# A fused attention and feed-forward kernel: the scores' bias product on 64 rows instead of 6, its query side held per tile of 128 tokens, and the planned order worked out again

## The chip, the cores and the metric

One core of one Trainium2 chip. The metric is device microseconds of one execution; the median of three executions of the kernel before is 662.76 us (662.45 to 664.29). PE is TensorE (its weight loads are told apart as PEld), DVE VectorE, ACT ScalarE, POOL GpSimd, SP SyncE, which here issues every DMA.

## What is computed

Causal attention with a forget bias, then two feed-forward layers with gates. The parts that matter, cut from the reference:

```python
# q, k, v: (4, 8, 576, 64), s: (4, 8, 576)
scores = scale * np.matmul(q, k.transpose(0, 1, 3, 2))
cum = np.cumsum(np.maximum(s, 0.0), axis=-1)
bias = -(cum[:, :, :, None] - cum[:, :, None, :])
scores = np.where(causal, -1000000000.0, scores + np.minimum(bias, 0.0))
attn = np.exp(scores - np.max(scores, axis=-1, keepdims=True))
attn = attn / (np.sum(attn, axis=-1, keepdims=True) + 1e-09)
x = np.matmul(attn, v)           # as (4 * 576, 512)
h = x @ w_in                     # 512 -> 1024
solu = h * softmax(h)            # then a layer norm times g_ln
y = ln(solu) @ w_out             # 1024 -> 512
h2 = np.maximum(np.maximum(y @ w1, y @ w2), y @ w3)   # 512 -> 768
out = h2 @ w_out2                # 768 -> 512
```

Products are made of f16 parts: a high and a low part of each side, three products of the four.

## The kernel before

Four batches go in two pairs; a pair has nine tiles: four blocks of 128 tokens of either batch (j = 0 to 3, batch c = 0 or 1), and one tile with the last 64 tokens of both, the tail. So there are 18 tiles, 0 to 17; tiles 8 and 17 are the tails. Two tiles make a group for the later layers, nine groups.

A tile goes through these steps. `prep` loads k, q and v, splits them into high and low halves (L417 and L419 the high half, L446 or on POOL L453 and L456 the low) and turns them, by DMA (L756, L766) or, for tiles 0 to 3, by TensorE with an identity (L486, L500). `scores` makes the scores of two heads at a time: head y of a pair uses rows 64y to 64y + 63 of TensorE, so the two run side by side. One step of it is the bias product (L832, both heads), and then three combinations of halves (L838). The bias is a product of 6 rows: three bf16 parts of the cumulative sum of the query side with ones, and ones with three parts of the key side. These rows stand in two buffers, `ckr` and `cqr`, of 128 x 4 x 576 bf16, at partitions 32c + 64y; both are filled with ones (or minus ones) by DVE (L557, L558) and then get their sums by DMA from `cum_d` (L596), eight loads a pair. A block of j = 0 has four steps in a row, of j = 1 two, of j = 2 and 3 one; a tail step makes four bias products, of 64 columns of weights each. Then come the minimum with the mask (L871, L906 in the tail), the exponential (L925), its halves (`es`), their turn by DMA (L952) into `et`, and `values` (L1009, in the tail L990 and L996), which ends in the scaling by the sums (L1043, L1037). Its result is split (`xs`) and turned (L1058) into `xt`.

`m1` is the product with w_in (L1082) and the normalisation (L1096, L1103, L1108, L1118, L1143 or L1144), which ends in halves `ln` and their turn (L1157) into `lnt`; buffers `e` and `ln` are single. `m2` is the product with w_out (L1179) and its two halves (L466 or L470, L1196), `m3` that with w1, w2, w3 and their maximum (L1218, L1237), `m4` that with w_out2 (L1252). The weights come as f32, are unpacked by DVE (L635, L641, L644) and split (L649, L659), which fills the first 150 us.

What sets the order: `Schedule.run` places every step on its engine with costs in ns, priorities `pos` made from the numbers in `P`, and a margin `look` within which the step of the lowest `pos` goes first. A step that can run on several engines goes where it would end first, by the margins in `spare`. The result is one fixed order for each engine; on the chip each engine takes its instructions in that order and waits by semaphores. Scores are forced into tile order (`in_turn`).

Of the kernel before, what the change touches and what calls it, by code (L numbers as in the profile page):

```python
# [32 lines left out]
P = dict(  # L33
    la=5.252,
    lp=-0.709,
    lu=-11.55,
    lv=-1.294,
    o1=-4.074,
    o2=-1.718,
    o3=-1.083,  # L40
    o4=-1.501,
    ds=2.623,
    wi=-17.396,
    wid=2.725,
    wo=-21.919,
    wod=-17.446,
    w3=14.089,
    w3d=1.947,
    w4=-21.45,
    w4d=16.108,  # L50
    mp=-2.793,
    look=[0.0, 0.0, 0.0, 1442.9, 54.8],
    spare=[1764.9, 1665.2, 1829.4, -777.9, -220.5, 1692.7, 26.2],
# [308 lines left out]
def build(nc, T, X, dims):  # L362
# [165 lines left out]
    def prologue():  # L528
# [29 lines left out]
        op([("DVE", 1100, lambda: nc.vector.memset(T["cqr"].bitcast(F32), MINUS_ONES))], [], ["cq1"], p0, kind="one")  # L558
# [29 lines left out]
    def load_c(p):  # L588

        unit(f"c{p}", f"c{p}")  # L590
        cd = T["cum_d"].rearrange("(b x y) i s -> b y i x s", b=B, y=2) if T else None
        for c in range(2):
            for name, of, n in (("ckr", "ck", 3), ("cqr", "cq", 0)):
                for y in range(2):
                    r0 = c * 32 + y * 64 + n
                    o = op([("SP", 450, lambda name=name, c=c, y=y, r0=r0: nc.sync.dma_start(  # L596
                        out=T[name][r0:r0 + 3], in_=cd[2 * p + c, y]))],
                       ["cum_d", of + "1"], [(of, c, y)], p * (2 * NB + 1) - P["la"] - P["lc"] + c * 0.2, dma=300, kind="c")
                    named[f"c{p}{c}"] = o
# [206 lines left out]
    def scores(t, h0):  # L806
# [73 lines left out]
        for n, (lo, hi) in enumerate(((0, KH), (KH, S))):  # L880
# [3 lines left out]
            def f_sc(n=n, lo=lo, hi=hi, sc=sc):  # L884
                steps = []
                for y in range(2):
                    for i in range(2):
                        cs = slice(i * 64, (i + 1) * 64)

                        def keys(x, r, i=i):  # L890
# [413 lines left out]
def fox_attention_solu_max3_kernel(  # L1304
# [110 lines left out]
```

## Time and profile before

| | |
|---|---|
| median of three executions | 662.76 us |
| the profiled execution: span | 661.9 us |
| PE busy | 620.3 us (94%) |
| DVE busy | 467.5 us (71%) |
| ACT busy | 299.6 us (45%) |
| POOL busy | 33.7 us (5%) |
| mean granted TensorE clock | 0.994 of full speed |

The page comes from one execution under the hardware profiler. Busy time of an engine is the union of its instructions' durations; products on PE are pipelined, so one that follows another starts before that one has ended. What a product costs the stream is therefore read from start to start. A row of a timeline merges neighbouring instructions of one kind: `x6` are six of them, and its duration runs from the start of the first to the end of the last. The number behind an idle engine's row is how long it was idle, and which instruction ended that.

### The profile page before, as it was taken

Reading aid. Unit: us, or ns where it says so; the run is one execution under the profiler, and the core shown is the slowest. Engines: PE = TensorE matmul, PEld = TensorE weight load, DVE = VectorE, ACT = ScalarE, POOL = GpSimd, SP = SyncE. Lnnn points to the kernel's source line nnn. Section 1 sums busy time; section 2 is a strip of 40 time slices with the busy share of each in tenths; the row PEclk is TensorE's granted clock in tenths of the full one; section 3 lists DMA queues with packets and bytes.
Section 4 is the critical chain, followed back from the end, with each engine's and each line's share of the span. In section 5 each row is a group of like instructions: output and inputs, shape, how many; then the busy total and the mean of one; then the engine's idle time right before and its main releaser. Section 6 shows DMA issues by size and latency. Waiting matters only on the chain.

```text
span 661.9 us, 15252 instructions
## 1 busy us (share of the span) xinstructions
PE 620.3 (94%) x6203; PEld 444.2 (67%) x6203; DVE 467.5 (71%) x1112; ACT 299.6 (45%) x712; POOL 33.7 (5%) x49
## 2 busy tenths in 40 slices
PE   3688978799999999999999999999999999999997
PEld 1344447577685567777577847785778577878684
DVE  7799999997697978696887668576884754513031
ACT  4687875464445555354743247325532514110100
POOL 1011100020000011020010001000000000000000
PEclk9999989899999999999999999999999999999999
DMA  6996866569988777898799674537663552100001
GB/s 171 279 248 163 207 192 172 163 111 173 176 158 135 148 129 129 132 142 164 142 195 173 129 130 105 94 72 112 124 102 65 109 69 49 34 33 1 33 1 32
DMA packets 249349, 82.66 MB, mean 125 GB/s; under 512 B 225472, under 2 KB 244096, under 8 KB 249280
## 3 DMA queue, kind: packets, MB, share of 16 engines
q1 hardware_dynamic: 249280, 81.70, 61.0%
q8 instruction: 48, 0.79, 0.5%
q14 instruction: 21, 0.17, 0.1%
HBM read 35.95 MB, written 4.83 MB: 62 GB/s over the span
## 4 chain that ended last, share of the span: by engine, by line
PE 71%; DVE 16%; issue 6%; DMA 3%; ACT 3%; SPq 0%; POOL 0%; DVEq 0%; POOLq 0%
PE acc L1218 27%; PE acc L1179 12%; PE acc L1252 10%; PE w L1082 9%; PE w L838 5%; PE av L1009 3%; DVE acc L641 2%; PE w L832 2%; DVE acc L644 2%; PE av L996 2%; DMA kt<-in_moe_w_in_dram 1%; DMA et<-es 1%; DVE r L871 1%; DVE f L635 1%; DVE w_h L659 1%
## 5 line engine op out<-in xcount | busy, mean ns | idle before, releaser
L1218 PE MATMUL acc<-x2A,w_h 128*128 128x256 f16 x1296 | 216.7, 274 | 3.2 <-DVE f L1237 1.1
L1218 PEld LDWEIGHTS <-w_h 128*128 128x128 f16 x1944 | 188.2, 98 | 32.9 <-issue 8.2
L1218 PE MATMUL acc<-x2B,w_h 128*128 128x256 f16 x648 | 177.2, 273 | 0.2 <-DVE x2B L1196 0.2
L925 ACT ACTIVATE r<-r,mn 128x128 f32<-128x128 f32 (+4 forms) x144 | 83.0, 578 | 59.4 <-DVE mn L871 48.2
L1082 PE MATMUL w<-w_in_h,xt 128*128 128x512 f16 x432 | 100.0, 383 | 1.4 <-DVE mn L871 1.2
L1179 PE MATMUL acc<-lnt,w_out_h 128*128 128x256 f16 x864 | 98.0, 273 | 1.0 <-DVE w_h L659 0.9
L1179 PEld LDWEIGHTS <-w_out_h 128*128 128x128 f16 x864 | 83.6, 98 | 13.1 <-issue 2.7
L1237 DVE TENSOR_TENSOR f<-f,acc 128x512 f32<-128x512 f32 x54 | 36.9, 683 | 68.0 <-PE acc L1218 68.0
L1082 PEld LDWEIGHTS <-xt 128*128 128x128 f16 x432 | 41.7, 98 | 50.1 <-issue 4.3
L1252 PE MATMUL acc<-w2o_h,h2A 128*128 128x512 f16 x216 | 64.4, 380 | 0.0
L446 DVE SCALAR_TENSOR_TENSOR es<-r,es 128x512 f16<-128x512 f32 (+1 forms) x89 | 59.8, 676 | 6.3 <-ACT es L417 4.6
L466 ACT ACTIVATE f<-acc 128x512 f32<-128x512 f32 x37 | 22.1, 596 | 85.5 <-PE acc L1218 51.6
L871 DVE CUSTOM_DVE_ANT_0 r<-w,mask 128x128 f32<-128x128 f32 (+3 forms) x128 | 57.7, 484 | 1.5 <-PE w L838 0.2
L838 PE MATMUL w<-kt,qt 64*128 64x256 f16 (+2 forms) x768 | 47.1, 262 | 0.2 <-ACT qt L503 0.2
L1103 ACT ACTIVATE ln<-e,st 128x1024 f32<-128x1024 f32 x18 | 20.7, 1147 | 49.8 <-DVE e L1096 44.5
L1252 PE MATMUL acc<-w2o_h,h2B 128*128 128x512 f16 x108 | 40.9, 379 | 0.0
L1009 PEld LDWEIGHTS <-et 128*128 128x128 f16 x960 | 34.7, 99 | 6.8 <-DMA et<-es 1.4
L1009 PE MATMUL av<-vs,et 128*128 128x64 f16 x960 | 36.4, 194 | 1.4 <-DMA et<-es 1.0
L838 PEld LDWEIGHTS <-qt 64*128 64x128 f16 (+1 forms) x864 | 26.6, 99 | 13.5 <-issue 6.4
L466 ACT ACTIVATE x2A<-acc 128x512 f16<-128x512 f32 x17 | 10.1, 595 | 55.0 <-PE acc L1179 55.0
L1252 PEld LDWEIGHTS <-h2A 128*128 128x128 f16 x216 | 19.6, 98 | 22.5 <-issue 2.1
L417 ACT ACTIVATE es<-r 128x512 f16<-128x512 f32 (+1 forms) x39 | 22.3, 575 | 23.9 <-DMA et<-es 20.9
(142 smaller groups left out, 730.9 us busy)
## 6 DMA issues: line engine op xcount, KB each, us to landing
kt<-in_moe_w_dram SPq DMA_DIRECT2D x18, 256.0 KB
vs<-in_moe_w_dram SPq DMA_DIRECT2D x18, 256.0 KB
raw<-in_k_dram SPq DMA_DIRECT2D x16, 256.0 KB
raw<-in_q_dram SPq DMA_DIRECT2D x16, 256.0 KB
raw<-in_v_dram SPq DMA_DIRECT2D x16, 256.0 KB
out_dram<-f SPq DMA_DIRECT2D x16, 256.0 KB
kt<-in_moe_w_out_dram SPq DMA_DIRECT2D x7, 512.0 KB
vs<-in_moe_w_out_dram SPq DMA_DIRECT2D x7, 512.0 KB
```

The source lines that it names most:

```text
L417: eng.activation(out=out(g), in_=src(g), func=AF.Copy, scale=sc(g))
L446: nc.vector.scalar_tensor_tensor(out=lo(g), in0=src(g), scalar=sc1(g), in1=hi(g), op0=ALU.mult, op1=ALU.subtract)
L466: nc.scalar.activation(out=out(*a), in_=in_(*a), func=AF.Copy, scale=scale)
L838: yield lambda n=n, qa=qa, o=o, kx=kx: nc.tensor.matmul(out=out()[:, o], lhsT=qv()[r, qa * HP + hp, ts], rhs=kx, start=False, stop=(n == 2 ...
L871: nc.vector.tensor_tensor_reduce(out=gw(R)[:, g], in0=gw(sc[y])[:, g], in1=T["mask"][:, SM - W:SM], scale=1.0 / S_MUL, scalar=3e38, op0=AL ...
L925: nc.scalar.activation(out=gw()[:, g], in_=gw()[:, g], func=AF.Exp, bias=mnf()[:, g:g + 1], scale=-1.0, accum_out=den(hs[g]),)
L1009: nc.tensor.matmul(out=out, lhsT=ea_[:, ea, kb], rhs=T["v_s"][c, kb // 2][:, kb % 2, ha + a, va], start=(kb == 0 and m == 0), stop=(kb == ...
L1082: nc.tensor.matmul(out=hb()[:, n * 512:(n + 1) * 512], lhsT=xt()[:, xa, kk], rhs=T["w_in_h"][:, wa, kk, n * 512:(n + 1) * 512], start=(kk ...
L1179: nc.tensor.matmul(out=ps()[:, d % 2 * GN:(d % 2 + 1) * GN], lhsT=T["w_out_h"][:, wa, kk, d * 128:(d + 1) * 128], rhs=lnt()[:, la, kk], st ...
L1218: nc.tensor.matmul(out=ps()[:, f % 2 * GN:(f % 2 + 1) * GN], lhsT=T["w123_h"][:, w, wa, f, kk], rhs=x2(xa)[:, kk], start=(kk == 0 and i == ...
L1237: op([("DVE", dve2(2 * GN), lambda ps=ps: nc.vector.tensor_tensor(out=m(), in0=m(), in1=ps(), op=ALU.max))], pk + [m], [m], pos, kind="m3x")
L1252: nc.tensor.matmul(out=ps(), lhsT=h2(ha)[:, f, o * 128:(o + 1) * 128], rhs=T["w2o_h"][:, wa, f], start=(f == 0 and i == 0), stop=(f == KF2 ...
```

## The change

The cumulative sums of the query side no longer stand for all 576 tokens of a pair. There are two buffers, `cq0` and `cq1`, one for each batch c of the pair, of 128 x 4 x 128 bf16. At the start POOL fills each with zeros, and rows 32c + 64y to 32c + 64y + 5 with minus ones. `load_cq` loads the three rows of sums for one tile: 128 tokens, or 64 in the tail; there are 40 such loads in place of 8. The bias product then takes rows 64y to 64y + 63 of `cq` and of `ckr`, 64 rows where it took 6; the rows beyond the six meet zeros. The planner's cost of a score step is 45 ns less, and all numbers in `P` that set the order are others, so that every engine's order differs from the old one. Of the steps that can run on several engines, POOL gets none any more.

```diff
-    look=[0.0, 0.0, 0.0, 1442.9, 54.8],
-    spare=[1764.9, 1665.2, 1829.4, -777.9, -220.5, 1692.7, 26.2],
+    look=[142.7, 33.8, 109.5, 156.1, 586.9],
+    spare=[1975.6, 1776.4, 6995.8, -4053.9, 1618.5, 1839.7, 112.3],
...
-        op([("DVE", 1100, lambda: nc.vector.memset(T["cqr"].bitcast(F32), MINUS_ONES))], [], ["cq1"], p0, kind="one")
+        for c in range(2):
+            op([("POOL", 400, lambda c=c: nc.gpsimd.memset(T["cq"][c].bitcast(F32), 0.0))],
+               [], [("cq", c, y) for y in range(2)], p0, kind="one")
+            for y in range(2):
+                r0 = 32 * c + 64 * y
+                op([("POOL", 400, lambda c=c, r0=r0: nc.gpsimd.memset(T["cq"][c][r0:r0 + 6].bitcast(F32), MINUS_ONES))],
+                   [], [("cq", c, y)], p0, kind="one")
...
+    def load_cq(t, pos):
+        p, c, j = tiles[t]
+        cd = T["cum_d"].rearrange("(b x y) i s -> b y i x s", b=B, y=2) if T else None
+        n = TL if c is None else 128
+        for i in ((0, 1) if c is None else (c,)):
+            for y in range(2):
+                r0 = i * 32 + y * 64
+                op([("SP", 450, lambda i=i, y=y, r0=r0: nc.sync.dma_start(
+                    out=T["cq"][i][r0:r0 + 3, :, 0:n], in_=cd[2 * p + i, y][:, :, j * 128:j * 128 + n]))],
+                   ["cum_d"], [("cq", i, y)], pos, dma=60, kind="cq")
...
             qb, qr, qk = load_tok("q", p, c, j, pos)
+            if j:
+                load_cq(t, pos)
...
             r = slice(64 * y, 64 * y + 64)
-            cr = slice(c0, c0 + 6)
             yield lambda: nc.tensor.matmul(
-                out=out(), lhsT=T["cqr"][cr, hp, cs], rhs=T["ckr"][cr, hp, ck], start=True, stop=False,
+                out=out(), lhsT=T["cq"][i][r, hp, 0:ts.stop - ts.start], rhs=T["ckr"][r, hp, ck], start=True, stop=False,
...
-            o = op([("PE", G * (pe(1, W) + pe(3 * nf, W / nf) + 60), f_sc)],
+            o = op([("PE", G * (pe(1, W) + pe(3 * nf, W / nf) + 15), f_sc)],
...
-    T["cqr"] = mk("cqr", [128, HP, S], BF16)
+    T["cq"] = [mk(f"cq{c}", [128, HP, 128], BF16) for c in range(2)]
```

How the order moves, at three places. The lines of the changed kernel stand some 20 further on: its L972 is the old L952, L777 the old L756, L742 the old L723, L1016 the old L996, L1102 the old L1082, L1238 the old L1218.

DVE at the very start, before and then after (`ckr` and `cqr` are the bias buffers, `k_tail` holds the identity there, `ln`, `e` and `lnt` the cumulative sums):

```order
L557 MEMSET ckr 128x1152
L558 MEMSET cqr 128x1152
L550 TENSOR_SCALAR k_tail<-k_tail 128x128 x5
L574 SCALAR_TENSOR_TENSOR e_106<-ln_107 32x576
L583 CAST lnt_108<-e_106 32x576
L582 TENSOR_TENSOR ln_107<-e_106,lnt_108 32x576
```

```order
L557 MEMSET ckr 128x1152
L550 TENSOR_SCALAR k_tail<-k_tail 128x128 x5
L580 SCALAR_TENSOR_TENSOR e_107<-ln_108 32x576
L589 CAST lnt_109<-e_107 32x576
L588 TENSOR_TENSOR ln_108<-e_107,lnt_109 32x576
```

The fill of the query side's buffer is gone from DVE; the sums follow one instruction sooner.

SP at the turns of tile 4's exponentials (`es` to `et`), before and then after; `raw` is what k, q and v are loaded to, `kt` the turned keys:

```order
L952 DMA_TRANSPOSE et_99<-es_93 128x6x128
L952 DMA_TRANSPOSE et_100<-es_94 128x6x128
L756 DMA_TRANSPOSE kt_71<-st_87 128x8x128
L723 DMA raw_84<-in_q_dram 128x8x64
L952 DMA_TRANSPOSE et_97<-es_93 128x6x128
L952 DMA_TRANSPOSE et_98<-es_94 128x6x128
```

```order
L972 DMA_TRANSPOSE et_100<-es_94 128x6x128
L972 DMA_TRANSPOSE et_101<-es_95 128x6x128
L742 DMA raw_85<-in_k_dram 128x8x64
L616 DMA cq_79<-cum_d 3x4x128 x2
L972 DMA_TRANSPOSE et_100<-es_94 128x6x128
L972 DMA_TRANSPOSE et_101<-es_95 128x6x128
L742 DMA raw_86<-in_q_dram 128x8x64
```

Two loads of the query side's sums, for tile 6, now stand between two pairs of turns.

PE behind the last values of tile 17, the last tile (`av` the values, `xt` the turned result of a tile, `w` the scores or the first layer, `acc` with `w_h` the three-way layer), before and then after:

```order
L996 LDWEIGHTS et_98
L996 MATMUL av_127<-vs_75,et_98 128x64
L1082 LDWEIGHTS xt_103
L1082 MATMUL w_126<-w_in_h,xt_103 128x512
...
L1218 LDWEIGHTS w_h
L1218 MATMUL acc_130<-x2A_110,w_h 128x256
```

```order
L1016 LDWEIGHTS et_99
L1016 MATMUL av_128<-vs_75,et_99 128x64
L1238 LDWEIGHTS w_h
L1238 MATMUL acc_130<-x2A_111,w_h 128x256
...
L1102 LDWEIGHTS xt_105
L1102 MATMUL w_127<-w_in_h,xt_105 128x512
```

Before, nine products of tile 16's first layer and 72 of the three-way layer stood ahead of tile 17's own first layer; after, 66 of the three-way layer.

## Rows read from the trace of the kernel before

**Rows 1.** the page, part 1: busy us (share of the span), xinstructions

```profile
PE 620.3 (94%) x6203; PEld 444.2 (67%) x6203; DVE 467.5 (71%) x1112; ACT 299.6 (45%) x712; POOL 33.7 (5%) x49
```

**Rows 2.** busy us in two stretches of the span, granted clock, DMA share, GB/s

```profile
0.00:150.00 150.00, 117.36 (x945) 74.03 (x946) 138.39 (x327) 100.36 (x236) 13.71 (x24) 0.98 0.71 190
150.00:540.00 390.00, 385.65 (x4290) 279.18 (x4289) 293.69 (x723) 180.66 (x440) 20.00 (x25) 1.00 0.74 131
```

**Rows 3.** the same for DVE alone, the densest ten microseconds

```profile
110.00:120.00 10.00, 9.96 (x20) 1.00 0.75 226
```

**Rows 4.** the chain of work that ended last: start us, us, what

```profile
625.97 23.58 PE acc L1218 x216
552.85 5.18 PE w L1082 x24
```

**Rows 5.** timeline of PE and its weight loads, four score steps: start us, us

```profile
318.60 0.28 PE L832 MATMUL w<-ckr,cqr 6*128 6x256 bf16 x2
318.81 0.50 PE L838 MATMUL w<-kt,qt 64*128 64x256 f16 x6
318.81 0.22 PEld L838 LDWEIGHTS <-qt 64*128 64x128 f16 x6
319.24 0.28 PE L832 MATMUL w<-ckr,cqr 6*128 6x256 bf16 x2
...
321.19 0.39 PE L1252 MATMUL acc<-w2o_h,h2A 128*128 128x512 f16 x1
```

**Rows 6.** timeline of PE near 59 us, f16 then f32 products

```profile
58.64 0.81 PE L1082 MATMUL w<-w_in_h,xt 128*128 128x512 f16 x3
59.28 0.60 PE L486 MATMUL acc<-k_tail,r 128*128 128x128 f32 x4
```

**Rows 7.** all of L832 from 150 us: count, ns min/median/max, starts, forms

```profile
L832 PE MATMUL w<-ckr,cqr x150: 224/318/385, 154.2 to 524.4; 6*128 6x512 bf16 x32, 6*64 6x256 bf16 x32, 6*64 6x320 bf16 x32, 6*128 6x384 bf16 x22
```

**Rows 8.** timeline of DVE, the fill of cqr

```profile
2.32 1.02 DVE L558 MEMSET cqr<- 128x1152 f32 x1 [0.19 <-issue]
```

**Rows 9.** timelines of POOL and SP; SP waits (total us, times, longest)

```profile
1.68 0.53 POOL L559 MEMSET mask<- 128x512 bf16 x1
13.21 0.59 SPq L596 DMA_DIRECT2D cqr<-cum_d  x2
SPq L952 <- DVE es L446: 70.3, 39, 10.6
```

**Rows 10.** timelines, tiles 17 and 7: last values on PE, issue of the turn

```profile
542.53 0.51 PE L996 MATMUL av<-vs,et 128*128 128x64 f16 x12
545.15 1.23 SPq L1058 DMA_TRANSPOSE xt<-xs  x1
248.82 0.78 PE L1009 MATMUL av<-vs,et 128*128 128x64 f16 x21
254.79 2.07 SPq L1058 DMA_TRANSPOSE xt<-xs  x1
```

**Rows 11.** the chain again: a turn from issue to landing

```profile
236.65 5.17 DMA et<-es
```

**Rows 12.** timelines: normalisation of tiles 5 and 17 to its turn; a landing

```profile
204.68 5.34 PE L1082 MATMUL w<-w_in_h,xt 128*128 128x512 f16 x24 [0.30 <-DVE mn L871]
232.77 1.71 SPq L1157 DMA_TRANSPOSE lnt<-ln  x1
558.06 1.22 DVE L1096 TENSOR_SCALAR_CACHE_REDUCE e<-w 128x1024 f32<-128x1024 f32 x1 [2.03 <-PE w L1082]
556.06 17.05 SPq L1157 DMA_TRANSPOSE lnt<-ln  x2
307.82 1.83 SPq L1157 DMA_TRANSPOSE lnt<-ln  x1
312.22 1.15 ACT L1103 ACTIVATE ln<-e,st 128x1024 f32<-128x1024 f32 x1 [5.27 <-DMA lnt<-ln]
```

**Rows 13.** waits of PE from 140 to 540 us: total, times, longest

```profile
PE w L832 <- DVE mn L906: 1.6, 1, 1.6
```

More of the change, by code (lines that the diff above doesn't have):

```diff
@@ L33 @@
 P = dict(
[L34 to L51, printed above, removed]
-    look=[0.0, 0.0, 0.0, 1442.9, 54.8],
-    spare=[1764.9, 1665.2, 1829.4, -777.9, -220.5, 1692.7, 26.2],
+    la=5.521,
+    lp=0.734,
+    lu=-45.556,
+    lv=1.446,
+    o1=-4.25,
+    o2=-2.859,
+    o3=-1.764,
+    o4=-1.319,
+    ds=0.164,
+    wi=-18.597,
+    wid=4.919,
+    wo=-12.688,
+    wod=-49.697,
+    w3=31.312,
+    w3d=5.865,
+    w4=-18.789,
+    w4d=42.619,
+    mp=-1.752,
+    look=[142.7, 33.8, 109.5, 156.1, 586.9],
+    spare=[1975.6, 1776.4, 6995.8, -4053.9, 1618.5, 1839.7, 112.3],
     n_st=4,
@@ L59 @@
     nr=3,
-    lat=2.304,
-    tp=0.396,
+    lat=2.777,
+    tp=0.872,
     wp=[0, 20, 20],
-    lc=-23.373,
+    lc=-35.216,
     S=[],
@@ L591, in load_c @@
         cd = T["cum_d"].rearrange("(b x y) i s -> b y i x s", b=B, y=2) if T else None
+        t = p * (2 * NB + 1)
         for c in range(2):
[L593 to L599, printed above, removed]
+            pos = t - P["la"] - P["lc"] + c * 0.2
+            for y in range(2):
+                r0 = c * 32 + y * 64 + 3
+                op([("SP", 450, lambda c=c, y=y, r0=r0: nc.sync.dma_start(out=T["ckr"][r0:r0 + 3], in_=cd[2 * p + c, y]))],
+                   ["cum_d", "ck1"], [("ck", c, y)], pos, dma=300, kind="c")
+            load_cq(t + c, pos)
+            named[f"c{p}{c}"] = S_.ops[-1]
+    def load_cq(t, pos):
[3 more added lines that the diff above has]
+        for i in ((0, 1) if c is None else (c,)):
+            for y in range(2):
+                r0 = i * 32 + y * 64
+                op([("SP", 450, lambda i=i, y=y, r0=r0: nc.sync.dma_start(
+                    out=T["cq"][i][r0:r0 + 3, :, 0:n], in_=cd[2 * p + i, y][:, :, j * 128:j * 128 + n]))],
+                   ["cum_d"], [("cq", i, y)], pos, dma=60, kind="cq")
     stage_keys = [
@@ L760, in prep @@
         qb, qr, qk = load_tok("q", p, c, j, pos)
+        if j:
+            load_cq(t, pos)
         qa = buf("st")
@@ L825, in scores, with products @@
         keyed = [(x, i, y) for x in ("ck", "cq") for i in ((0, 1) if tail else (c,)) for y in range(2)]
-        def products(out, y, h, ts, cs, keys, c0, ck):
+        def products(out, y, h, ts, keys, i, ck):
             hp = h // 2
             r = slice(64 * y, 64 * y + 64)
-            cr = slice(c0, c0 + 6)
             yield lambda: nc.tensor.matmul(
-                out=out(), lhsT=T["cqr"][cr, hp, cs], rhs=T["ckr"][cr, hp, ck], start=True, stop=False,
+                out=out(), lhsT=T["cq"][i][r, hp, 0:ts.stop - ts.start], rhs=T["ckr"][r, hp, ck], start=True, stop=False,
                 skip_group_check=True,
@@ L894, in f_sc @@
                         steps.append(products(
-                            lambda y=y, cs=cs: sc[y]()[cs, 0:hi - lo], y, h0 + y, cs, slice(SM, S),
-                            keys, 32 * i + 64 * y, slice(lo, hi),
+                            lambda y=y, cs=cs: sc[y]()[cs, 0:hi - lo], y, h0 + y, cs, keys, i, slice(lo, hi),
                         ))
```

3 lines of the change are left out of this document (1 added, 2 removed).

## The prediction

> **What bounds the kernel now.** I read the page first, then the busy times by stretch, then the chain of waits, then TensorE's timeline. PE is busy 94% of the 661.9 us, DVE 71%, ACT 45% [rows 1]. By stretch this splits in two [rows 2]: up to 150 us PE is busy 117.4 us and DVE 138.4, and in the densest ten microseconds there DVE has no gap left (9.96 of 10) [rows 3], because it unpacks the weights; from 150 to 540 us PE is busy 385.7 of 390 us and DVE only 293.7. So the front is DVE's and the rest is PE's, and a microsecond taken from PE's stream after 150 us is a microsecond of the end.
>
> A busy PE is not a PE at full rate, so I need its rate when nothing disturbs it. In the chain 216 products of 256 columns take 23.58 us, 0.109 each, and 24 of 512 columns take 5.18 us, 0.216 each [rows 4]. Now the scores. In one stretch four steps follow each other [rows 5]; a step is a pair of bias products (L832, 6 rows, one for each of two heads, side by side) and three pairs of L838 (64 rows). From 318.60 to 321.19 they take 2.59 us, 0.648 a step. Four undisturbed slots of 256 columns are 0.436. Each step loses 0.212, at two places: between the bias pair and L838 (318.60 to 318.81, against a slot of 0.109), and between L838 and the next bias pair. One change of row height, 6 to 64 or back, costs 0.106 us.
>
> **The change, part by part.**
>
> *Bias product on 64 rows.* The products stay as many and as wide, only the row height is now that of L838. What a bias pair then costs is not in this trace. Bounds: a plain slot (0.109, as between pairs of L838), or today's 0.21 with its drain. I take the plain slot, because L838's own pairs alternate between different weights on the same 64 rows and lose nothing. One difference is left between the two kinds: the bias is bf16, L838 f16. The nearest row is a change of type at one row height, L1082 (f16) to L486 (f32): three products of 512 columns start at 58.64, the next kind at 59.28, 0.64 for three slots of 0.216 [rows 6]; no loss. So the drain belongs to the rows, not to the type.
>
> Count: the 150 bias products after 150 us [rows 7] are 43 pairs and, in the two tails, 16 steps of four, 59 steps. In PE's order they stand in 35 unbroken stretches, so 59 changes 6 to 64 go, and 24 changes 64 to 6 inside stretches; entry from and exit to 128 rows stay, one each per stretch (the new order has 44 stretches in all, as the old). 83 x 0.106 = **8.8 us**, all in PE's part. The same sum for the 21 steps before 150 us is 33 x 0.106 = 3.5 us, but DVE sets the time there, so I book nothing for it.
>
> A page of the Trainium skill speaks against the edit: "TensorE: Matmul & The Clock Gate", Part 3, says that a weight load overlaps running products only when its row group differs. By that the bias weights, now in the rows of L838, would load in the open. The trace disagrees for L838 itself, which loads within its own rows: six loads done in 0.22 us under six products of 0.50 us [rows 5]. By the page the saving would be smaller (a rival below).
>
> *Sums of the query side per tile, zeroed.* Removed: DVE's fill of cqr, 1.02 us at the start [rows 8]. Added on POOL: two fills of 128x256 f32 and four of 6 rows. POOL's fill of 128x512 bf16, as many bytes, takes 0.53 us [rows 9]; from 0 to 0.53 each, the six are at most 3.2 us behind POOL's first work and done by about 7 us, before the loads that need them are issued (13.21 us for the old ones, [rows 9]). Without that cover the first scores would start later by what is missing. Added on SP: 32 more small loads (40 for 8). Two issues of the old ones take 0.59 us [rows 9], so 9.4 us in all, of a queue that waits 70.3 us for one line of DVE alone [rows 9]. Each waits until the scores two tiles before have read the buffer. What stands behind one in SP's queue is most often a pair of turns of exponentials (L952); in the new order the values that need these come 11 us of PE work or more after the score step that the load waits for. No cost.
>
> *The order worked out anew.* (a) Front: the DVE instructions ahead of the first L1237 are the old ones less net 1.3 us by their rows' durations (mostly the fill). Ahead of the sixth (end of the first group's L1218) they are 6.8 us less, but PE has then done 3.1 us less, so 3.7 net. Between 0 and 5 us, I take **2 us gained**. (b) Of the exponentials' 128x512 high halves 27 of 36 go from DVE to ACT, and POOL's share of such work to both. ACT has 209 us free of 390 [rows 2]. No cost. (c) PE's covers. From the last values of a tile to its L1082 the program goes through L1043, the split and a turn by DMA (L1058). In the new order nine tiles leave only 7.2 to 8.3 us of PE work there (tile 17: 66 L1218 of 0.109); the old order left 8.9 or more everywhere. The turn is issued 2.1 us after the last value of tile 17 (543.04 to 545.15), and 5.2 us after that of tile 7, for which DVE was late (249.60 to 254.79); the median of 14 tiles is 3.4 [rows 10]. A turn lands 4.4 to 5.2 us after its issue starts [rows 11, 12]. So 6.5 to 10.4 us; with 3.4 + 4.4 = 7.8 each of nine waits 0 to 0.6, about 2 us together. (d) Last group: from its last L1082 to its L1179 stand 99 L1218 and 30 L1252, 17.3 us. Today the way of that tile ran from 558.06 to the issue of its turn at about 571.3 (the second of two, ended at 573.11), 13.3, and such a turn lands 4.4 after (307.82, ACT goes on at 312.22) [rows 12]: 17.7, a wait of 0.4. (e) The old order's largest wait after 150 us is 1.6 for a score buffer [rows 13]; covers from scores to values were 9.3 us at least and are now 12.2, so I book 1.4 of its waits as gone. (c) to (e): **+1 us**, from -4 to +9.
>
> Sum on the profiled execution: 661.9 - 8.8 - 2 + 1 = 652.1. The median of the runs stands 0.9 above that span, so 653.0.
>
> **Rivals.** *The new covers are too short.* The drains go, but half of the nine turns come as late as that of tile 7: 5.2 + 4.4 = 9.6 against 7.7 of cover, 1.9 each, 4.5 x 1.9 = 8.6 in place of 2. Time 653.0 + 6.6 = 659.6. For it: all nine are tight at once. Against: DVE has less to do than before.
>
> *Bias on 64 rows drains as before*, for a reason that no row shows. Then only front and waits: 661.8. Against it stands [rows 6].
>
> *Loads in the open.* 59 steps each show one load: six take 0.22 us overlapped [rows 5], so about 0.09 each alone, 5.3 back, 658.3. This is the result of the page named above.
>
> *Slower: the first product after normalisation waits.* L1179 of groups 2, 3 and the last has 17.7, 19.0 and 17.3 us of cover; the old order gave the first two 27.9 and 30.1. Tile 5 today took from 210.02 to 232.77 until its turn was issued, 22.8, since it queued behind tile 4 on a single buffer [rows 12]. As late as this, 27.2 with landing, the three wait 9.5, 8.2 and 9.9: 27.6 us, 680.6. It decides from 11.8 us in sum, 4 each; I put it at half of the full price, 667. Against: in the new order these tiles' L1082 stand 27 us or more from the tile before, not 7.
>
> *More than forecast.* Front 5, no new waits, old ones gone: 645.
>
> **How the numbers follow.** Forecast (646 to 658) 0.68; short covers 0.13; drain stays 0.05; loads in the open 0.03; slower 0.08; more 0.03. About 0.3% (2 us) is what a measurement of this kernel can tell from no change, so same is 660.8 to 664.8. Faster: 0.68 + 0.03 + 0.03 + 0.08 of the short covers = 0.82. Same: 0.05 of them + 0.05 = 0.10. Slower 0.08. The range 645 to 660.5 holds forecast, loads in the open and most of the short covers.
>
> **What the profile after would show.** Drains: a step of 256 columns inside a stretch takes 0.436 and not 0.648. Front: the sixth L1237 starts 3 us or more earlier. Covers: waits of PE before L1082 for a turn under 1 us each. SP: no turn held up behind a load of cq until PE needs it. I am wrong if bias and L838 still stand 0.21 apart at 256 columns, or if PE waits more than 9 us in sum after 150 us.

## The result, and the profile after

The kernel after takes 652.88 us (median of 4, 652.53 to 653.85) where the kernel before takes 663.52 (4 runs, 662.45 to 665.38): ratio 0.9831, 95% interval 0.9805 to 0.9857. The forecast was 653.0. The number was right and two terms of its sum were wrong, in opposite directions. The span of the profiled execution is 652.1 us.

Part 1 of the page after, and its stretches (columns as in [rows 1] and [rows 2]); the third stretch is one that the prediction did not look at, with the row of before below it:

```profile
PE 608.0 (93%) x6203; PEld 447.2 (69%) x6203; DVE 451.4 (69%) x1083; ACT 328.4 (50%) x767; POOL 5.1 (1%) x18
```

```profile
0.00:150.00 150.00, 112.16 (x907) 74.00 (x907) 132.08 (x313) 96.61 (x226) 5.13 (x18) 0.99 0.70 186
150.00:540.00 390.00, 388.33 (x4241) 290.29 (x4240) 277.46 (x683) 208.01 (x493) 0.00 (x0) 1.00 0.70 127
20.00:40.00 20.00, 10.28 (x74) 6.09 (x75) 12.12 (x37) 9.58 (x28) 0.00 (x0) 1.00 0.59 187
```

```profile
20.00:40.00 20.00, 14.69 (x100) 7.63 (x97) 18.14 (x61) 15.37 (x44) 2.46 (x3) 1.00 0.98 289
```

Between 20 and 40 us every engine does less than before: DVE 12.1 us for 18.1, and the DMA engines are busy 0.59 for 0.98. The timelines of PE and DVE after show why. The first scores, which began at 17.49 before, wait until 23.79 for a load of `ckr` (in brackets: idle time and what ended it), and the second head of the pair until 25.23. DVE, whose next work in its order is the minimum of these scores, stands idle for 8.1 us.

```profile
23.79 0.26 PE L854 MATMUL w<-ckr,cq 64*128 64x128 bf16 x1 [10.05 <-DMA ckr<-cum_d]
25.23 0.26 PE L854 MATMUL w<-ckr,cq 64*128 64x128 bf16 x1 [1.18 <-DMA ckr<-cum_d]
```

```profile
27.25 0.29 DVE L892 CUSTOM_DVE_ANT_0 r<-w,mask 128x128 f32<-128x128 f32 x1 [8.13 <-PE w L860]
...
30.22 0.69 DVE L663 SCALAR_TENSOR_TENSOR acc<-kt,acc 128x512 int32<-128x512 int32 x1
```

SP's timeline after, the same time:

```profile
12.91 0.64 SPq L603 DMA_DIRECT2D ckr<-cum_d  x2
13.64 0.56 SPq L616 DMA_DIRECT2D cq<-cum_d  x2
...
20.13 0.30 SPq L603 DMA_DIRECT2D ckr<-cum_d  x1
20.53 0.33 SPq L636 DMA_DIRECT2D kt<-in_moe_w_out_dram  x1
20.91 0.31 SPq L603 DMA_DIRECT2D ckr<-cum_d  x1
21.31 0.26 SPq L616 DMA_DIRECT2D cq<-cum_d  x1
21.67 0.36 SPq L636 DMA_DIRECT2D vs<-in_moe_w_out_dram  x1
26.73 0.90 SPq L616 DMA_DIRECT2D cq<-cum_d  x3
30.93 0.36 SPq L636 DMA_DIRECT2D kt<-in_moe_w_in_dram  x1
```

The four loads for the scores of batch 0 are issued by 14.2. The two heads begin 3.7 and 4.3 us after the issues at 20.13 and 20.91, which are the key-side sums of batch 1. From 22.0 to 26.7 SP stands at a load of `cq` for tile 2, which waits until tile 0's scores have read the buffer. The next weights, issued at 30.93, wait for something else: the buffer they go to is free only when DVE's L663 on it ends, at 30.91. So it is DVE's idle time that makes the weights late.

Later the profile is as forecast. Four steps of scores of 256 columns (timelines of PE and of its weight loads, to be read beside [rows 5]):

```profile
345.09 0.28 PE L854 MATMUL w<-ckr,cq 64*128 64x256 bf16 x2
345.21 0.49 PE L860 MATMUL w<-kt,qt 64*128 64x256 f16 x6
345.54 0.27 PE L854 MATMUL w<-ckr,cq 64*128 64x256 bf16 x2
345.65 0.49 PE L860 MATMUL w<-kt,qt 64*128 64x256 f16 x6
345.98 0.27 PE L854 MATMUL w<-ckr,cq 64*128 64x256 bf16 x2
```

```profile
345.43 0.10 PEld L854 LDWEIGHTS <-cq 64*128 64x128 bf16 x2
345.54 0.32 PEld L860 LDWEIGHTS <-qt 64*128 64x128 f16 x6
```

A step takes 0.44 us (345.09 to 345.54, to 345.98), where it took 0.648. The two loads of bias weights are done at 345.53, while products of L860 on the same rows run. And these are all waits of PE after 150 us (total, times, longest), 1.7 us; before, the one of [rows 13] alone was 1.6:

```profile
PE w L854 <- DVE mn L926: 0.5, 1, 0.5
PE av L1029 <- DMA et<-es: 0.5, 1, 0.5
PE acc L1199 <- ACT lnt L503: 0.4, 1, 0.4
PE w L854 <- DVE mn L892: 0.3, 1, 0.3
```

To set runs beside each other I split PE's time in two. A product has a slot, the time to the next start when nothing disturbs it: 0.109 us for 256 columns and 0.216 for 512 [rows 4], narrower ones in proportion to 256 and those between on the line. An f32 product counts twice its columns (the four of 128 columns in [rows 6] start 0.109 apart), and products that run side by side count as one slot, also where they start apart. Every kernel here has the same products, 574.6 us of slots. *Done by 150 us* is the sum of the slots of what PE has started by then, and *lost after 150 us* is the time from there to the last start that the remaining slots do not fill. The spans of two kernels thus differ by what one of them lost more and had done less. Before, 92.1 and 24.6; after, 90.5 and 13.2. b64_early and the five runs on it that follow change nothing before 150 us, and what they have done by then ranges from 92.5 to 93.8: so much the figure moves from one execution to the next.

| run | bias rows | order | first scores, us | done by 150 us | lost after 150 us | median, us | ratio to before (95%) |
|---|---|---|---|---|---|---|---|
| before | 6 | old | 17.49 | 92.1 | 24.6 | 663.5 to 665.3 | 1 |
| after | 64 | new | 23.79 | 90.5 | 13.2 | 652.88 | 0.9831 (0.9805 to 0.9857) |
| a6 | 6 | new | 17.59 | 94.4 | 20.9 | 656.90 | 0.9882 (0.9858 to 0.9907) |
| a_early | 64 | new, two loads moved | 17.50 | 97.7 | 12.2 | 645.97 | 0.9721 (0.9695 to 0.9747) |
| b64 | 64 | old | 25.07 | 89.0 | 20.9 | 663.23 | 0.9983 (0.9965 to 1.0001) |
| b64_early | 64 | old, two loads moved | 18.09 | 93.8 | 20.5 | 658.30 | 0.9908 (0.9886 to 0.9931) |
| ae_eh | 64 | a_early, 38 steps to DVE | | 97.1 | 13.6 | 647.37 | 0.9737 (0.9717 to 0.9757) |
| b64e_eh | 64 | b64_early, 43 steps to ACT | | 93.6 | 21.2 | 659.04 | 0.9912 (0.9889 to 0.9935) |
| b64e_all | 64 | b64_early, 123 steps moved | | 93.1 | 25.4 | 662.29 | 0.9973 (0.9957 to 0.9990) |
| b64e_cover | 64 | b64_early, five places | | 92.5 | 21.0 | 658.87 | 0.9924 (0.9901 to 0.9946) |
| b64e_port | 64 | b64_early, two steps off POOL | | 93.1 | 24.0 | 662.15 | 0.9971 (0.9955 to 0.9988) |
| b64e_port2 | 64 | the same, turns later | | 92.8 | 19.3 | 658.21 | 0.9904 (0.9874 to 0.9934) |
| a_dbl_early | 64 | a_early, two buffers of `cq` | 17.67 | 97.3 | 12.3 | 645.48 | 0.9710 (0.9691 to 0.9729) |
| a_first | 64 | a_dbl_early, first loads earlier | 14.90 | 98.3 | 12.2 | 645.38 | 0.9730 (0.9704 to 0.9757) |

The expectations below speak of smaller lost times (22.8 for before, 18.2 for a6, 15.3 for b64_early, 18.8 for b64e_port): there, products of a pair that start more than 30 ns apart had passed for two slots.

### The profile page after: what moved, and what is told of

It reads as the page before. It is cut to its first block, busy times and chain, and to the rows that moved or that the text cites. A ratio compares the mean times of both kernels' runs of the same rounds, so it can differ in the third digit from the quotient of the medians.

```text
span 652.1 us, 15319 instructions
## 1 busy us (share of the span) xinstructions
PE 608.0 (93%) x6203; PEld 447.2 (69%) x6203; DVE 451.4 (69%) x1083; ACT 328.4 (50%) x767; POOL 5.1 (1%) x18
## 4 chain that ended last, share of the span: by engine, by line
PE 81%; DVE 11%; DMA 3%; issue 2%; ACT 2%; SPq 1%; DVEq 0%
PE acc L1238 31%; PE acc L1199 13%; PE w L1102 12%; PE acc L1272 11%; PE w L860 4%; PE av L1029 3%; DVE acc L660 3%; PE w L854 2%; DVE acc L663 2%; PE av L1016 2%; PE acc L486 1%; DVE f L654 1%; DVE w_h L678 1%; DMA kt<-in_moe_w_in_dram 1%; DMA et<-es 1%
## 5 line engine op out<-in xcount | busy, mean ns | idle before, releaser
L1238 PE MATMUL acc<-x2A,w_h 128*128 128x256 f16 x1296 | 214.4, 273 | 2.2 <-DVE f L1257 1.5
L1238 PEld LDWEIGHTS <-w_h 128*128 128x128 f16 x1944 | 188.0, 98 | 27.8 <-issue 4.0
L1238 PE MATMUL acc<-x2B,w_h 128*128 128x256 f16 x648 | 176.8, 273 | 0.0
L1102 PE MATMUL w<-w_in_h,xt 128*128 128x512 f16 x432 | 100.2, 381 | 0.3 <-ACT xt L503 0.3
L1199 PE MATMUL acc<-lnt,w_out_h 128*128 128x256 f16 x864 | 98.6, 273 | 0.4 <-ACT lnt L503 0.4
L1199 PEld LDWEIGHTS <-w_out_h 128*128 128x128 f16 x864 | 83.4, 98 | 13.3 <-issue 1.5
L446 DVE SCALAR_TENSOR_TENSOR es<-r,es 128x512 f16<-128x512 f32 (+1 forms) x92 | 58.2, 638 | 24.0 <-ACT es L417 23.8
L1102 PEld LDWEIGHTS <-xt 128*128 128x128 f16 x432 | 41.6, 98 | 47.4 <-issue 2.6
L1257 DVE TENSOR_TENSOR f<-f,acc 128x512 f32<-128x512 f32 x54 | 37.0, 686 | 45.6 <-PE acc L1238 45.3
L417 ACT ACTIVATE es<-r 128x512 f16<-128x512 f32 (+1 forms) x73 | 42.8, 592 | 40.5 <-DMA et<-es 34.8
L860 PE MATMUL w<-kt,qt 64*128 64x256 f16 (+2 forms) x768 | 45.0, 262 | 0.0
L1116 DVE TENSOR_SCALAR_CACHE_REDUCE e<-w 128x1024 f32<-128x1024 f32 x18 | 22.0, 1223 | 31.7 <-PE w L1102 31.7
L860 PEld LDWEIGHTS <-qt 64*128 64x128 f16 (+1 forms) x864 | 33.9, 102 | 5.8 <-issue 1.3
L854 PE MATMUL w<-ckr,cq 64*128 64x128 bf16 (+5 forms) x192 | 25.7, 308 | 12.0 <-DMA ckr<-cum_d 11.2
```

Of the source, the lines that this page charges most:

```text
L417: eng.activation(out=out(g), in_=src(g), func=AF.Copy, scale=sc(g))
L446: nc.vector.scalar_tensor_tensor(out=lo(g), in0=src(g), scalar=sc1(g), in1=hi(g), op0=ALU.mult, op1=ALU.subtract)
L854: yield lambda: nc.tensor.matmul(out=out(), lhsT=T["cq"][i][r, hp, 0:ts.stop - ts.start], rhs=T["ckr"][r, hp, ck], start=True, stop=False, ...
L860: yield lambda n=n, qa=qa, o=o, kx=kx: nc.tensor.matmul(out=out()[:, o], lhsT=qv()[r, qa * HP + hp, ts], rhs=kx, start=False, stop=(n == 2 ...
L1102: nc.tensor.matmul(out=hb()[:, n * 512:(n + 1) * 512], lhsT=xt()[:, xa, kk], rhs=T["w_in_h"][:, wa, kk, n * 512:(n + 1) * 512], start=(kk ...
L1199: nc.tensor.matmul(out=ps()[:, d % 2 * GN:(d % 2 + 1) * GN], lhsT=T["w_out_h"][:, wa, kk, d * 128:(d + 1) * 128], rhs=lnt()[:, la, kk], st ...
```

## The experiments: rows, order, and the late first scores

The theory for the late start: the product that takes 64 rows of `ckr` reads the rows of both batches, so it waits for both batches' key-side loads, though zeros of `cq` take batch 1's rows out of the result. The rival: the new order of SP's loads.

**a6**, the kernel after on 6 rows:

```diff
-                out=out(), lhsT=T["cq"][i][r, hp, 0:ts.stop - ts.start], rhs=T["ckr"][r, hp, ck],
+                out=out(), lhsT=T["cq"][i][32 * i + 64 * y:32 * i + 64 * y + 6, hp, 0:ts.stop - ts.start],
+                rhs=T["ckr"][32 * i + 64 * y:32 * i + 64 * y + 6, hp, ck],
```

> The kernel after with the bias product on its 6 rows again; sums per tile, their loads and the whole order stay as in after. My theory has two parts. (1) The drains come back: 83 changes of 0.106 after 150 us, +8.8. (2) The late first scores of after (23.79 and 25.23 us for the two heads, 17.49 before) come from the 64 rows themselves: the product now also reads the rows of the pair's other sequence, whose key-side loads are issued at 20.13 and 20.91, so it waits for them. With 6 rows the first scores start by 18.5 with no load moved, and VectorE's idle time of 7.9 us between 20 and 40 us shrinks by 5 or more: 652.9 + 8.8 - (2 to 7) = 655 to 660. Rival A, the first loads are late because they stand behind two weight loads in SP's new order: first scores still at 23 or later, and with the front's own drains the time is 661 to 665. Rival B, SP is held up by the per-tile load of tile 2 first and the scores are late for that: first scores also unchanged.

656.90 us, inside the range of the theory. PE's timeline in a6:

```profile
17.59 0.44 PE L854 MATMUL w<-ckr,cq 6*128 6x128 bf16 x2 [4.00 <-DMA cq<-cum_d]
```

and SP's there:

```profile
20.59 0.30 SPq L603 DMA_DIRECT2D ckr<-cum_d  x1
21.00 0.33 SPq L636 DMA_DIRECT2D kt<-in_moe_w_out_dram  x1
21.37 0.31 SPq L603 DMA_DIRECT2D ckr<-cum_d  x1
```

The scores begin 3.0 us before the first of batch 1's loads is even issued, with SP's order as in after. Rivals A and B fall. DVE's idle time between 20 and 40 us goes from 7.9 to 3.6 us, 4.3 less and not the 5 or more expected.

**a_early**, after with batch 1's key-side loads behind batch 0's:

```diff
     sched.run()
+    od = sched.order
+    late = [o for o in od if o.unit == "c0." and o.kind == "c"][2:]
+    for o in late:
+        od.remove(o)
+    at = max(i for i, o in enumerate(od) if o.unit == "c0." and o.kind == "c")
+    od[at + 1:at + 1] = late
```

> The kernel after with two loads moved in SP's order and nothing else: the key-side sums of the first pair's other sequence go directly behind those of its first sequence, ahead of the loads they stood behind. Theory (the 64-row product reads both sequences' rows): the first scores start at 17 to 18.5 instead of 23.79/25.23, SP is no longer held at 22.0 to 26.7, the transfers no longer stop at 27 to 32 us, and since VectorE sets the time there, 3 to 7 us of the end are gained: 646 to 650. Rival A (place behind the weight loads of the first sequence's own sums): first scores not earlier than 22, time 652 to 653.5. Rival C, the front's lateness is made up before 150 us anyway, since VectorE is short of work later: first scores early, time within 1 us of 652.9.

645.97 us, 6.9 below after. PE's and DVE's timelines, and the stretch from 20 to 40 us, in a_early:

```profile
17.50 0.45 PE L854 MATMUL w<-ckr,cq 64*128 64x128 bf16 x2 [4.50 <-DMA cq<-cum_d]
```

```profile
19.70 0.29 DVE L892 CUSTOM_DVE_ANT_0 r<-w,mask 128x128 f32<-128x128 f32 x1 [1.30 <-PE w L860]
```

```profile
20.00:40.00 20.00, 14.80 (x96) 8.08 (x95) 17.23 (x52) 15.49 (x41) 0.00 (x0) 1.00 0.93 274
```

Two loads of 13.5 KB at another place give back DVE's 5 us of work in that stretch. The first minimum starts 7.5 us earlier than in after (19.70 for 27.25), and 6.9 of these reach the end; rivals A and C of this run fall.

**b64** and **b64_early**, the kernel before in its own order on 64 rows, without and with the same two loads moved (of b64, the core; b64_early adds the move shown above):

```diff
-                out=out(), lhsT=T["cqr"][cr, hp, cs], rhs=T["ckr"][cr, hp, ck], start=True, stop=False,
+                out=out(), lhsT=T["cq"][c0 // 32 % 2][r, hp, cs], rhs=T["ckr"][r, hp, ck], start=True, stop=False,
...
-    T["cqr"] = mk("cqr", [128, HP, S], BF16)
+    T["cq"] = [mk(f"cq{c}", [128, HP, 256], BF16) for c in range(2)]
...
         for o in sched.order:
...
             o.fn()
+            t = int(o.unit[1:-1]) if o.kind == "ldq" else 0
+            p, j, c = t // 9, t % 9 // 2, t % 2 ^ t // 9
+            if j == 0 or t in seen:
+                continue
...
+                    nc.sync.dma_start(
+                        out=T["cq"][i][r0:r0 + 3, :, j % 2 * 128:j % 2 * 128 + n],
+                        in_=cd[2 * p + i, y][:, :, j * 128:j * 128 + n])
```

> The kernel before, in its own order, with the bias product on 64 rows; the zero-padded query-side sums lie in two buffers per sequence and the load of a tile goes directly behind the load of its queries, so no load waits for a score. One part of the change alone. Drains: -8.8 after 150 us and up to -3.5 before. Theory on the front: the first product waits here too for the other sequence's loads, which this order issues at 17.84 to 21.4, so first scores at about 25 instead of 17.49, 3 to 7 us lost: 663.5 - 8.8 - (0 to 3.5) + (3 to 7) = 654 to 662. Rival (no such wait): first scores at 17.5, 651 to 655. If the drain did not belong to the rows: 663 or more.

663.23 us: nothing gained. The first scores come at 25.07, as the theory says. The time is over its range, and by the time alone the last case of the expectation, a drain that does not belong to the rows, would fit as well. PE's timelines decide it, of the first score steps before and in b64:

```profile
17.49 0.29 PE L832 MATMUL w<-ckr,cqr 6*128 6x128 bf16 x2
18.14 0.29 PE L832 MATMUL w<-ckr,cqr 6*128 6x128 bf16 x2
```

```profile
25.64 0.39 PE L833 MATMUL w<-ckr,cq 64*128 64x128 bf16 x2
26.07 0.39 PE L833 MATMUL w<-ckr,cq 64*128 64x128 bf16 x2
```

A step takes 0.43 us for 0.65, two changes of row height less. The saving of 64 rows is there (lost 20.9 for 24.6), and the wait that they bring eats it (done 89.0 for 92.1).

> As the run before it (the kernel before in its own order, bias product on 64 rows), with the two key-side loads of the other sequence moved directly behind those of the first. Theory: first scores at about 17.5 again, and the change of rows alone is left: 663.5 - 8.8 - (0 to 3.5) = 651 to 655. If the time is that of after (652.9) or below, the new order brought nothing of its own; if it is 2 us or more above, the order brought the rest. Rival (waits at the score buffers take back what the drains gave): 656 to 660.

658.30 us, 4.9 below b64, 3.3 above the upper end of the theory and inside the rival's range. The drains are gone, but of their 8.8 us only 4.1 left the lost time (24.6 to 20.5). 3.0 came back as longer waits of PE for `et` and for score buffers (4.2 us in sum after 150 us before, 7.2 here), the rest in pieces that I did not name. In the new order, from a6 to a_early, it was 8.7 of 9.1 (20.9 to 12.2; 85 changes there hold 9.3, with a wait of 0.25 among them). The new order is thus worth 3.7 us of lost time on 6 rows (24.6 to 20.9) and 8.3 on 64 (20.5 to 12.2). What in it does that?

## The experiments: what the new order does after 150 us

**ae_eh** and **b64e_eh** exchange the engine of the exponentials' high halves, at their places in the sequence, in either direction:

```diff
+    moved = {'s11.0': [0], 's11.4': [0], 's12.0': [1], 's12.4': [1], 's13.0': [0], 's13.2': [0],
...
+             's8.6': [0, 1], 's9.0': [0, 1]}
+    seen = {}
+    for o in sched.ops:
+        if o.kind == "eh":
+            n = seen[o.unit] = seen.get(o.unit, -1) + 1
+            if n in moved.get(o.unit, ()):
+                o.fn = [f for e, ns, f in o.alts if e == "DVE"][0]
```

> The kernel a_early (after with the two loads moved, 645.97) with one thing put back as before: the 38 high halves of exponentials after 150 us that the new order gives to ScalarE and the old one gave to VectorE go to VectorE again, at the same place of the sequence. Theory: TensorE's waits after 150 us that the new order took away (4.6 us between the kernel before and the run with 6 rows: 22.8 against 18.2 us lost) came from VectorE, which before had the score minima and these halves in one queue; so 2 to 5 us of waits before products of scores and of values come back, 648 to 651. Rival: the sequence of TensorE's work (covers of 12 us from scores to values in place of 9) took them away: under 1 us lost, 645.5 to 647.

647.37 us, between the two forecasts; lost time 12.2 to 13.6.

> The other direction: the run b64_early (old order, 64 rows, 658.3) with 43 high halves of exponentials after 150 us given to ScalarE, as in after, at their old places. Theory (they burden VectorE): TensorE's lost time after 150 us falls from 15.3 by 2 to 5 us, 653 to 656. Rival (sequence): 657 to 659.5, or longer where ScalarE's queue now delays the exponentials themselves.

659.04 us: the rival. Lost time 20.5 to 21.2.

**b64e_all**, the same with every step whose engine differs:

```diff
+    moved = {('h1.0', 'm3c', 0): 'DVE', ('h1.0', 'h2h', 0): 'ACT', ('h1.2', 'h2h', 0): 'DVE',
...
+    for o in sched.ops:
+        k = o.unit, o.kind
+        n = seen[k] = seen.get(k, -1) + 1
+        e1 = moved.get(k + (n,))
+        if e1:
+            o.fn = [f for e, ns, f in o.alts if e == e1][0]
```

> As the run before it, but all 123 operations after 150 us whose engine differs between the two orders go to the engine that they have in after (the 43 halves, the halves of tokens, of the normalised rows and of maxima, and GpSimd's 20 us of work, of which none is left); the sequence stays the old one. If engines are what the new order gains after 150 us: 651 to 655, and lost time near 9 us. If it is the sequence: 657 to 660. If only GpSimd's work, on a port that it shares with VectorE, is to blame, this run falls by 2 or more below the one with the 43 halves alone.

662.29 us, above both ranges and 4.0 above b64_early: the new engines in the old sequence are worse than the old ones, and without POOL's work nothing is gained on b64e_eh. Its profile has a granted clock of 0.91 between 250 and 270 us, which explains at most 1.8 of the 4.9 us of lost time above b64_early (25.4 for 20.5). So it is not the assignment by itself.

**b64e_cover** puts work in front of five waiting steps:

```diff
+    for kind, u, at, n in (("av", "v5.2", 0, 2), ("av", "v5.3", 0, 2), ("av", "v7.2", 0, 8), ("sc", "s8.4", 1, 5), ("sc", "s14.4", 0, 5)):
+        x = [o for o in od if (o.kind, o.unit) == (kind, u)][at]
+        i = od.index(x)
+        nxt = [o for o in od[i:] if o.eng == "PE" and o.kind in ("m2", "m3")][:n]
+        for o in nxt:
+            od.remove(o)
+        i = od.index(x)
+        od[i:i] = nxt
```

> The run b64_early (old order, 64 rows, 658.3, lost time after 150 us 15.3) with five places of TensorE's sequence changed: ahead of the products of values of tile 5 (third and fourth pair of heads) and of tile 7 (third pair), and ahead of the scores of the tail tile 8 (third pair, second half) and of tile 14 (third pair), stand the 2, 2, 8, 5 and 5 triples of products of L1180 or L1219 that came right behind. At these places TensorE waited 6.5 us in that run (0.69, 0.62 and 0.8, 1.17, 1.94, 1.58 with the score step of tile 6 behind the first). Theory (what the new order gave after 150 us is work in front of these steps, not other engines): 4 to 6 us of the waits go, 652.5 to 655. Rival (what they wait for hangs on TensorE's own earlier steps and moves along): under 1.5 us, 657 or more.

658.87 us: the rival, my theory of covers falls. Lost time 21.0 for 20.5. The wait of 1.17 us at the values of tile 7 is gone, and one of 1.15 stands at 277.17. The wait of tile 14's scores stayed 1.51 us (it was 1.58) with 1.6 us more work in front of it: what they wait for moved along. In b64_early, DVE, POOL and PE there:

```profile
403.22 0.55 DVE L872 CUSTOM_DVE_ANT_0 r<-w,mask 128x384 f32<-128x384 f32 x1
403.69 0.08 DVE L872 DVE_READ_ACCUMULATOR2_ANT mn<- 128x1 f32 x1
403.69 2.35 DVE L446 SCALAR_TENSOR_TENSOR h2B<-f,h2A 128x512 f16<-128x512 f32 x1
405.96 0.54 DVE L872 CUSTOM_DVE_ANT_0 r<-w,mask 128x384 f32<-128x384 f32 x1
```

```profile
403.37 2.13 POOL L456 TENSOR_TENSOR ln<-e,ln 128x1024 f16<-128x1024 f32 x1 [59.53 <-DVE h2A L419]
```

```profile
406.57 0.34 PE L833 MATMUL w<-ckr,cq 64*128 64x384 bf16 x2 [1.42 <-DVE mn L872]
```

A subtraction that takes DVE 0.69 us elsewhere takes 2.35 here, while POOL's runs; the minima behind it come 1.7 us late, and the scores wait for the buffer that they free. The kernel before has the same rows at 406.80 (2.35) and 409.68, and a second such place at 249.53.

**b64e_port** takes these two pieces from POOL and gives them to DVE, behind the minima:

```diff
     sched.run()
+    od = sched.order
+    for n, (unit, k) in (("n6", ("s8.4", 3)), ("n12", ("s14.4", 0))):
+        x = [o for o in od if o.kind == "lnl" and o.unit == n][0]
+        y = [o for o in od if o.kind == "lnT" and o.unit == n + "."][0]
+        x.fn = [f for e, ns, f in x.alts if e == "DVE"][0]
+        od.remove(x)
+        od.remove(y)
+        at = od.index([o for o in od if o.kind == "ttr" and o.unit == unit][k])
+        od[at + 1:at + 1] = [x, y]
```

> The run b64_early (old order, 64 rows, 658.3) with two of GpSimd's 25 pieces of work after 150 us taken from it: the low halves of the normalised rows of tiles 6 and 12 (2.12 us each) go to VectorE, behind the score minima that TensorE waits for, their turns with them. Theory: in b64_early a subtraction of VectorE that takes 0.69 us elsewhere takes 2.35 us at 248.68 and at 403.69, each time until GpSimd's instruction, begun 0.3 us before it, ends; the minima behind it come 1.7 us late, and TensorE waits 1.94 and 1.58 us for the score buffers at 252.49 and 406.57. Then both waits fall under 0.5 us, lost time after 150 us falls from 15.3 to 12 to 13, and the time to 655 to 656.5. Rival (VectorE is late there anyway, as the waits that stayed when work was put in front of them suggest): both waits stay above 1 us, 657.5 to 659.5.

662.15 us. The mechanism is right: both waits for score buffers are gone (0.28 us, and none). The time is 3.9 us worse: SP now stands at the turns of these rows until they are ready, and the turns behind are late. PE and SP in b64e_port:

```profile
265.01 0.23 PE L991 MATMUL av<-v_tail,ett 128*128 128x64 f16 x2 [2.42 <-DMA ett<-est]
```

```profile
257.48 1.92 SPq L1158 DMA_TRANSPOSE lnt<-ln  x1
259.52 3.05 SPq L953 DMA_TRANSPOSE et<-es  x2
262.62 1.24 SPq L960 DMA_TRANSPOSE ett<-est  x1
```

**b64e_port2** moves those two turns behind the stretch's own:

```diff
-        od[at + 1:at + 1] = [x, y]
+        od[at + 1:at + 1] = [x]
+        at = max(i for i, o in enumerate(od) if (o.kind, o.unit) == last)
+        od[at + 1:at + 1] = [y]
```

> The run b64e_port with the two turns of normalised rows further back in SP's order, behind the turns of exponentials of the same stretch (tile 8's, and the first two pairs of tile 14). In b64e_port the two waits for score buffers went from 1.94 and 1.58 to 0.28 and under 0.25, but SP stood at these turns until 257.48 and 413.26 and the turns behind it came 3.2 and 7.8 us later than in b64_early: TensorE waited 2.59 for them at 265.01 and 1.32 and 1.09 near 421. Theory: with the turns out of the way these go too and what is left is the gain of taking GpSimd's work away, lost time after 150 us 11.5 to 13.5 (15.3 in b64_early, 18.8 in b64e_port) and 654.5 to 657. Rival: VectorE's own 1.2 us for each half comes back as a wait elsewhere: lost time 15 or more, 658 to 660.

658.21 us, as b64_early: the rival. The turns' waits are gone too, but one for `et` of 2.2 us stands at 276.81 instead. Lost time is 19.3 for 20.5; in the time this does not show. Waits of PE from 150 to 560 us in b64e_port2:

```profile
PE av L997 <- DMA et<-es: 2.6, 2, 2.2
PE av L1010 <- DMA et<-es: 2.3, 4, 1.0
PE w L833 <- DVE mn L872: 0.9, 2, 0.6
```

So in the old sequence most of a wait that is taken away in one place comes back at the next tight one. Engines, work in front of a step, and POOL's two pieces, each alone, gave 1.4 us or nothing. That it is the sequence as a whole, or the sequence together with the engines, is what is left by elimination; no run shows it. Which of its places carry the 3.7 to 8.3 us stays open.

## The experiments: is there more to have

**a_dbl_early** gives each batch two buffers of `cq`, used in turn:

```diff
-                    out=T["cq"][i][r0:r0 + 3, :, 0:n], in_=cd[2 * p + i, y][:, :, j * 128:j * 128 + n]))],
+                    out=T["cq"][i][r0:r0 + 3, :, j % 2 * 128:j % 2 * 128 + n], in_=cd[2 * p + i, y][:, :, j * 128:j * 128 + n]))],
```

> The kernel a_early with the query-side sums in two buffers per sequence, used in turn by a sequence's tiles, so that the load of a tile no longer waits for the scores of the tile before it and holds up nothing in SP's queue. In a_early SP waits 4.4 us for scores at these loads before 150 us. If this hold-up still costs: 643 to 645.5. If SP's queue has slack there: 645.5 to 646.5.

645.48 us, not to be told from a_early (645.97). Once the first scores are in time, SP's stops at the loads of `cq` cost nothing.

**a_first** puts the first loads one place further ahead:

```diff
+    first = [o for o in od if o.unit == "c0." and o.kind == "c"] + [o for o in od if o.unit == "c0." and o.kind == "cq"][:2]
+    for o in first:
+        od.remove(o)
+    at = [i for i, o in enumerate(od) if o.unit == "w5." and o.kind == "wdma"][0]
+    od[at:at] = first
```

> The run a_dbl_early (645.48) with the first pair's sums, key side of both sequences and query side of the first, one place further ahead in SP's order, in front of the weight load that SP issues at 11.76 only because its buffer is unpacked by then. First scores wait for the query-side load there, issued last at 13.50, until about 18.0. If that wait reaches the end through VectorE, which waits 1.3 us for the first scores: first scores at 16 to 17, 644 to 645. If the weights are what VectorE waits for: 645 to 646.

645.38 us with first scores at 14.90: 2.8 us earlier, and no time gained. DVE then waits for weights instead. The best versions are 1.1% below the kernel after, and the move of two loads is all that it takes.

## Why the prediction was right, and where it was wrong

**The drains: right.** The 83 changes 6 to 64 and back cost 8.80 us in the kernel before (59 of 0.110, 24 of 0.097), against 8.8 in the sum, and none is left. The rivals "drains as before" and "loads in the open" fall by the same rows: a step takes 0.44 us, and the bias weights load under products on their own rows. The rule of the Trainium skill weighed in the prediction ("TensorE: Matmul & The Clock Gate", Part 3), that a weight load overlaps running products only where its row group differs, does not describe these loads. What the sum took for granted, that drains taken from PE reach the end, holds in the new order alone: in the old one 4.7 of the 8.8 stayed lost, 3.0 of it as longer waits.

**The drains of the front, booked at nothing: wrong.** Done by 150 us rises by 3.2 from a6 to a_early (94.44 to 97.66), which differ in the rows and in the place of two loads and have their first scores within 0.1 us of each other. In the old order the rise, from 92.1 to between 92.5 and 93.8, is hardly clear of the spread. That DVE sets the time there did not make PE's drains free: of the 3.5 us counted and not booked, most was there in the new order.

**The front's 2 us gained: wrong.** The sixth L1257 was to start 3 us earlier or more. DVE's timeline after, for which the kernel before has 148.00:

```profile
147.83 0.68 DVE L1257 TENSOR_TENSOR f<-f,acc 128x512 f32<-128x512 f32 x1
```

It starts 0.17 earlier, and PE has done 1.6 us less by 150 us, about the spread of that figure: nothing was gained. The estimate of the order itself was sound: a6 has that step at 143.29, 4.7 earlier (3.7 were worked out), and is 2.3 us ahead by 150 us. What failed is the step on the rows, "the products stay as many and as wide, only the row height is now that of L838": with the rows a product also takes their writers, batch 1's loads are late, and DVE, which sets the time there, waits 8.1 us for the first scores. That cost 7 us (after against a_early).

**Fills and loads.** POOL's six fills end at 4.4 us, so no cost, as said. The loads of `cq` on SP, "no cost" too: right. In the front SP stood at one for 4.7 us, but the weights behind it waited for DVE until 30.9, and a_dbl_early, where these loads wait for no scores, gains nothing on a_early.

**The covers: +2.4 us that did not come.** None of the nine tight covers waits more than 0.13 us. Timelines of PE and SP after for tile 17, one of the three with the shortest cover, 7.04 us (to be read beside [rows 10]):

```profile
574.18 0.51 PE L1016 MATMUL av<-vs,et 128*128 128x64 f16 x12
```

```profile
576.81 1.23 SPq L1078 DMA_TRANSPOSE xt<-xs  x1
```

```profile
581.74 0.81 PE L1102 MATMUL w<-w_in_h,xt 128*128 128x512 f16 x3
```

The turn is issued 2.1 us after the last value, and the median of the 14 tiles is 2.7 where I took 3.4 from the old order. With 4.4 to land that is 7.1, about the shortest cover. The rival "short covers" falls; so does the slower one, L1199 waiting 0.4 us in sum.

**The old order's waits: too small.** (c) to (e) were to add 1 us, with -4 as a bound. Without its drains the old order lost 15.8 us after 150 us (24.6 - 8.8), the new one 13.2: -2.6. I had counted 1.4 of its waits as gone; the kernel before lost 1.81 (the wait of [rows 13]) and 1.27 behind subtractions that POOL stretched, 1.15 for `et`, and the rest in pieces under 0.5. That all work leaves POOL stood in the prediction as "no cost" on ACT. What POOL's work did to DVE was not seen; what its leaving is worth by itself no run shows, and b64e_port2, which took away these two pieces, won no time.

**The sum.** Drains -8.8, front +1.6, waits -2.6: -9.8, as the spans, and as forecast. The forecast held by luck: the front's miss of 3.6 (2 gained, 1.6 lost) and the waits' miss of 3.6 (1 added, 2.6 gone) cancel.

## What to carry to other kernels

An operand padded to a full group of rows is read in full: before widening it, list who writes the added rows and when, since zeros on the other side take them out of the result and not out of the wait. A stall taken from the busiest engine reaches the end only where the sequence has no tight step left to take it back, so hold the order fixed and measure both, rows and order, by themselves. A total that comes out right is checked term by term.

## What the runs showed of the hardware

A change between 64 and 128 rows costs PE about 0.10 us as well: 0.096 us at the median of the 33 entries to scores and of the 34 exits after 150 us in the kernel after. A change between 6 and 64 rows costs 0.097 to 0.110. The page "TensorEngine Tiling (Array Packing)" of the Trainium skill, Tiling Modes, Key Properties, says that a change of tiling mode drains the engine, without a time; the traces agree.

At these places a subtraction of DVE with two inputs in SBUF, begun 0.3 us after an instruction of POOL that reads SBUF, takes 2.35 us for 0.69 and ends 0.54 us after POOL's (403.37 + 2.13 against 403.69 + 2.35). "SBUF — State Buffer" of the Trainium skill, Who interferes with whom, says that such a pair contends for shared ports and that the second to start blocks until the first ends. The traces agree. In the kernel before, two such places stand right ahead of waits of PE of 3.1 us in sum, though b64e_port2 did not win these back.

POOL's fill of 128x256 f32 took 0.31 to 0.34 us, less than the 0.53 of the bf16 fill of as many bytes [rows 9].
